# Residual block on one core: input transform for two channel blocks at a time, one more chunk by columns, single positions accumulated in the weight banks

## The chip, the core and the metric

The kernel runs on one core of one Trainium2 chip. A core has a matrix engine (TensorE, PE in the profile, with its weight loads as PEld), a vector engine (VectorE, DVE), an activation engine (ScalarE, ACT), a general engine (GpSimd, POOL) and a queue engine for transfers (SyncE, SP). They run side by side and wait for each other by semaphores. [...] The metric is the time of one execution on the device, in microseconds, as the median of several runs.

## What is computed

A residual block of a diffusion model, on two images of 512 channels and 64 x 64 points, in bf16:

```python
def conv3(z, w):
    zp = jnp.pad(z, ((0, 0), (0, 0), (1, 1), (1, 1)))
    taps = [jnp.einsum("bchw,oc->bohw", zp[:, :, i:i+H, j:j+W], w[:, :, i, j]) for i in range(3) for j in range(3)]
    return sum(taps)
h = conv3(silu(gn(x, g1, be1)), w1)          # gn: group norm, 4 groups of 128 channels
h = h + (silu(t_emb) @ w_emb).reshape(B, C, 1, 1)
h = conv3(silu(gn(h, g2, be2)), w2)
return x + h
```

Both convolutions have 512 input and 512 output channels: four blocks of 128 each way. "Layer one" and "layer two" below are the two convolutions.

## The kernel before

**Method.** Each convolution is done by a Winograd transform over rows: six rows of the input give six transformed rows (positions 0 to 5), and six products with transformed weights give four output rows. In the direction of columns there are two ways. By taps, a position is the sum of three matmuls per input block, one per column tap, each 512 columns wide (eight rows of 64). By columns, the row transform is followed by a second transform over pairs of columns: then a position is four products, each 256 wide, one matmul per input block. By taps a position takes 3 x 512 columns per input block, by columns 4 x 256.

**Tiling.** The 64 rows of an image make two chunks of 32 rows; with two images a layer has four chunks, numbered 1 to 4 here (idx 0 to 3 in the code). A *set* is one output block of one chunk: `one_set` (line 801), and `final_set` (line 747) for the very last. A set runs positions 1 and 3, then 0 and 5 (components 1 and 2), then 2 and 4, then the remaining components of 0 and 5; ACT evacuates each accumulator and DVE combines the results into the output rows `y`. Accumulators are three tiles `acc` of two banks each; two more banks, `xa` and `xb`, take the transposed weights. Positions 0 and 5 go by columns in all chunks but the first of layer one. Positions 1 and 3 go by columns in chunks 3 and 4 of layer two: `more_cols` (line 699) for chunk 3 and `more_pair` (line 734) for chunk 4.

**Input transform.** `v_block` (line 629) makes the transformed input V of one input block for one chunk. It loads the rows into one of two buffers `src`, ACT writes Silu of the normalised rows into one of two padded buffers `a_tmp` (rows of 66: a zero column on each side), and `make_v` (line 591) makes the positions: rows of 66 are read and written whole, so the sums have 1056 elements (2 x 8 x 66). For positions 0 and 5 by columns, one difference of 1024 and two sums of 512 that read every second element follow. `v_more_split` (line 557) and `v_more` (line 548) make the parts for positions 1 and 3 by columns. V has eight tiles, four per chunk in turn: the V of chunk n+2 is written when chunk n's sets are done.

**Weight transform.** `u_blocks` (line 493) loads weights, transposes them on PE into `xa` and `xb`, copies them out on ACT and makes the transformed weights U on DVE, in six sums per pair of blocks. `u_more` (line 475) turns the weights of positions 1 and 3 into those by columns, in place, after the last set that uses them by taps: now after chunk 2 of layer two.

**Order.** Nothing runs in program order. Every instruction is recorded with a cost and its dependencies, and a planner (class `_Plan`, line 25) makes one list per engine before the kernel is built, by forward and backward passes over the whole block with perturbed priorities; `STEPS` (line 31) lists the seeds of the perturbations that are kept. So the order of instructions on every engine can differ between two versions of the kernel even where the code is the same. Helper `tt` (line 316) records DVE's two-input operations and `act` (line 335) ACT's, which is why so many rows of the profile have lines L318 and L348; `groups` (line 659) records the matmuls (L667).

**Transfers.** SP issues loads, the store of layer one's output to memory (`h_scr`) and the stores of the result; POOL issues the transfers that add x to `y`.

Of the kernel before, what the change touches and what calls it, by code (L numbers as in the profile page):

```python
# [24 lines left out]
class _Plan:  # L25
# [5 lines left out]
    STEPS = ((0, 3), (500001, 2), (500002, 3), (500004, 3), (500005, 3), (500006, 3), (500007, 3), (500008, 2),  # L31
# [157 lines left out]
def kernel(  # L189
# [40 lines left out]
    COL0 = (1, 2, 3)  # L230
    SLOT = (1, 3, 2, 4, 0, 5)
# [30 lines left out]
    a_tmp = [sb([(CR + 2) * WP], f"a_tmp{i}") for i in range(2)]  # L262
    vt = sb([2, TR, 2, WP], "vt")
# [4 lines left out]
    Vbuf = [sb([VSZ], f"V{i}") for i in range(2 * CT)]  # L268
    src = [sb([(CR + 2) * W], f"src{i}") for i in range(2)]
    stage = [sb([CQ], f"stage{i}") for i in range(3)]  # L270
    stg = [sb([CR * W], f"y{i}") for i in range(3)]
    g1t = sb([TR * P], "g1t")
# [220 lines left out]
    def u_blocks(layer, ot, c0, loads, tmp=None, dve=False, act_scale=True):  # L493
# [4 lines left out]
        mid = slots(U, c0, n, S_MID, [[1, KP]])  # L498
        half = view(tmp, 0, [[KP, n], [1, KP]])
        up = lambda j: slots(U, c0, n, S_UP + NKX * j, [[1, KP]])  # L500
        for i, wn in enumerate(loads):
# [20 lines left out]
            copy(one(S_MID, 1), pb, "xb", KP, lambda t: t[:].rearrange("p k o -> p (k o)"))  # L522
        scaled(up(3), g(0), 0.25, act_scale and not dve)
        scaled(half, mid, 0.5, act_scale and not dve)
        tt(up(1), g(0), g(1), ALU.add)
        tt(up(0), up(1), mid, ALU.add)
        tt(up(1), up(1), mid, ALU.subtract)
        tt(up(3), up(3), g(1), ALU.add)
        tt(up(2), up(3), half, ALU.add)
        tt(up(3), up(3), half, ALU.subtract)  # L530
# [15 lines left out]
    more_buf = lambda ct: (a_tmp + src)[ct]  # L546

    def v_more(V, X):
        rows = lambda kx, st: view(V, kx, [[NI, 2], [WP, TR], [st, W // st]])
        dst = lambda o, n: view(X, o, [[n * TR, 2], [n, TR], [1, n]])  # L550
        tt(dst(0, W), rows(0, 1), rows(2, 1), ALU.subtract)
        tt(dst(4 * NC, W // 2), rows(1, 2), rows(2, 2), ALU.add)
        tt(dst(6 * NC, W // 2), rows(2, 2), rows(1, 2), ALU.subtract)

    spare = lambda ct: (stage + [g1t])[ct]

    def v_more_split(V, at, D):
        rows = lambda kx, st: view(at, kx, [[NI, 2], [WP, TR], [st, W // st]])
        tt(view(D, 0, [[W * TR, 2], [W, TR], [1, W]]), rows(0, 1), rows(2, 1), ALU.subtract)
        dst = lambda i: view(V, i * NI, [[NC, 2], [W // 2, TR], [1, W // 2]])  # L560
        tt(dst(0), rows(1, 2), rows(2, 2), ALU.add)
        tt(dst(1), rows(2, 2), rows(1, 2), ALU.subtract)

    def rhs_more_split(V, D, j, c):
        if c in (0, 3):
            return view(D, j * 2 * NC + (1 if c == 3 else 0), [[W, TR], [2, W // 2]])
        return view(V, (c - 1) * NI + j * NC, [[1, NC]])
# [4 lines left out]
    def rhs_row(V, pos, kx):  # L572
        return view(V, SLOT.index(pos) * NI + kx, [[WP, TR], [1, W]])

    def rhs_col(V, j, c, o=4 * NI):
        if c in (0, 3):
            return view(V, o + j * 2 * NC + (1 if c == 3 else 0), [[W, TR], [2, W // 2]])
        return view(V, o + (4 if c == 1 else 6) * NC + j * NC, [[1, NC]])

    def silu_rows(layer, b, ch, ct, res, at):  # L580
        rows = at[:].rearrange("p (r w) -> p r w", w=WP)
        r0 = ch * CR - 1
        lo, hi = max(r0, 0), min(r0 + CR + 2, H)
        for edge, r in ((ch == 0, 0), (ch == NCH - 1, CR + 1)):
            if edge:
                pool(lambda r=r: nc.gpsimd.memset(rows[:, r, 1:W + 1], 0.0), [], [rows[:, r, 1:W + 1]], cost=0.2)  # L586
        act(rows[:, lo - r0:hi - r0, 1:W + 1], res[:, lo * W:hi * W].rearrange("p (r w) -> p r w", w=W)
            if res.shape[1] == HW else res.rearrange("p (r w) -> p r w", w=W),
            func=ACT.Silu, bias=nb_all[layer, b][:, ct:ct + 1], scale=sc_all[layer, b][:, ct:ct + 1])

    def make_v(V, at, rs, col, on_act, split=False):
        n2 = 2 * NI
        q2 = view(vt, 0, [[2 * WP, TR], [1, 2 * WP]])
        s2 = view(vt, n2, [[2 * WP, TR], [1, 2 * WP]])
        s_, r_ = (view(vt, n2 + i * WP, [[2 * WP, TR], [1, WP]]) for i in range(2))
        qs, pr = (view(vt, i * WP, [[n2, 2], [2 * WP, TR], [1, WP]]) for i in range(2))
        rows2 = lambda j: view(at, j * WP, [[TH * WP, TR], [1, 2 * WP]])
        pair = lambda j, d: view(at, j * WP, [[d * WP, 2], [TH * WP, TR], [1, WP]])
        flat = lambda t, i: view(t, i * NI, [[WP, TR], [1, WP]])
        vv = lambda i: view(V, 2 * i * NI, [[NI, 2], [WP, TR], [1, WP]])  # L600
        scaled(q2, rows2(1), 4.0, on_act[0])
        tt(s2, rows2(3), rows2(1), ALU.subtract)
        tt(q2, q2, rows2(3), ALU.subtract)
        scaled(flat(rs, 0), r_, 0.25, on_act[1])
        scaled(flat(rs, 1), s_, -4.0, on_act[1])
        scaled(s_, s_, 2.0, on_act[2])
        if not split:
            tt(vv(0), pr, qs, ALU.add)
        tt(vv(1), pr, qs, ALU.subtract)
        if not col:  # L610
            w05 = view(V, 4 * NI, [[1, n2]])
            tt(view(V, 4 * NI, [[NI, 2], [WP, TR], [1, WP]]), pair(0, 5), pair(2, 1), ALU.subtract)
            tt(w05, w05, view(rs, 0, [[1, n2]]), ALU.add)
            return
        vt_, vo = (rs, n2) if split else (vt, 0)
        tt(view(vt_, vo, [[NI, 2], [WP, TR], [1, WP]]), pair(0, 5), pair(2, 1), ALU.subtract)
        if split:
            tt(view(at, 0, [[NI, 2], [WP, TR], [1, WP]]), pr, qs, ALU.add)
        w05f = view(vt_, vo, [[1, n2]])
        tt(w05f, w05f, view(rs, 0, [[1, n2]]), ALU.add)  # L620
        o = 4 * NI
        tt(view(V, o, [[W, 2 * TR], [1, W]]), view(vt_, vo, [[WP, 2 * TR], [1, W]]),
           view(vt_, vo + 2, [[WP, 2 * TR], [1, W]]), ALU.subtract)
        odd = view(vt_, vo + 1, [[WP, 2 * TR], [2, W // 2]])
        evn = view(vt_, vo + 2, [[WP, 2 * TR], [2, W // 2]])
        tt(view(V, o + 4 * NC, [[W // 2, 2 * TR], [1, W // 2]]), odd, evn, ALU.add)
        tt(view(V, o + 6 * NC, [[W // 2, 2 * TR], [1, W // 2]]), evn, odd, ALU.subtract)

    def v_block(layer, b, ch, ct, V, res=None, rs=None, on_act=(False, True, True)):
        at = a_tmp[count["v"] % 2]  # L630
        k = src[count["v"] % 2]
        count["v"] += 1
        r0 = ch * CR - 1
        lo, hi = max(r0, 0), min(r0 + CR + 2, H)
        if res is None:
            res = k[:, 0:(hi - lo) * W]
            from_h = layer == 1
            dma(res, (h_scr if from_h else x_v)[b, ct][:, lo * W:hi * W],
                reads=[f"h{b}{ct}{c}" for c in range(NCH)] if from_h else [], writes=[res])
        silu_rows(layer, b, ch, ct, res, at)  # L640
        split = layer == 1 and b * NCH + ch == len(chunks) - 2
        make_v(V, at, rs if rs is not None else k, is_col(layer, b, ch), (layer == 1,) + on_act[1:], split)
        if split:
            v_more_split(V, at, spare(ct))
# [33 lines left out]
    def row_pair(pair, U, V, gid):  # L678
        a = next_acc()
        todo = []  # L680
        for i, pos in enumerate(pair):
            for ct in range(CT):
                taps = [(u_tap(U[ct], pos, kx), rhs_row(V[ct], pos, kx)) for kx in range(NKX)]
                todo.append((i, a[:, i], [t[0] for t in taps], [t[1] for t in taps], 0.218 * NKX))
        groups(todo, a, (gid, pair))
        return a

    def col_pair(cc, U, V, gid, lead=0.0, js=(0, 1)):
# [3 lines left out]
        for j in js:  # L692
            for k, c in enumerate(cc):
                pairs = [(u_col(U[ct], j, c), rhs_col(V[ct], j, c)) for ct in range(CT)]
# [4 lines left out]
    def more_cols(U, V, gid):  # L699
        def cols(cc):  # L700
# [3 lines left out]
            for j in range(2):  # L704
                for k, c in enumerate(cc):
                    pairs = [(u_col_more(U[ct], j, c), rhs_more_split(V[ct], spare(ct), j, c)) for ct in range(CT)]
# [395 lines left out]
```

## Time and profile before

| | |
|---|---|
| median of 3 runs | 490.44 us (490.42 to 490.81) |
| profiled execution | 491.79 us |
| its span, first to last instruction | 489.7 us |
| mean granted clock of PE | 0.997 |
| busy: PE, weight loads, DVE, ACT, POOL | 481.4, 292.3, 459.6, 391.7, 46.7 us |
| chain of waits: PE, DVE, transfers | 91%, 5%, 2% |

How to read it: the busy time of an engine is the union of its instructions' records. Records of following instructions overlap, so that the time an instruction takes from its engine is read from start to start in the order of time, and not from its record. The slices show the busy share in forty equal parts of the span. The chain of waits is followed back from the last instruction to what released each step. In the groups, "x" is a count, and the numbers behind the bar are busy time, mean time of one in ns, and idle time of the engine just before them with what ended it.

### The profile page before, as it was taken

The page shows a single profiled execution, that of the slowest core. Times are in us where ns is not written, and L with a number is a line of the kernel's source. Part 1 is how long each engine was busy: PE and PEld are TensorE (multiplying, and loading weights), DVE is VectorE, ACT ScalarE, POOL GpSimd, SP SyncE. Part 2 cuts the span into 40 slices and gives each one's busy share as a digit, 9 for nine tenths or more (in the row PEclk, how much of TensorE's full clock was granted, in tenths as well). Part 3 has the DMA queues.
Part 4 walks back from the last instruction along what each step waited for, and adds up shares of the span by engine and source line. Part 5 has one row for each costly group of instructions (what it writes and reads, how often), then busy time and mean ns, then how long its engine had stood idle before and what let it go on. Part 6 is the DMA issues. An engine that isn't in the chain of part 4 may idle for free.

```text
span 489.7 us, 8717 instructions
## 1 busy us (share of the span) xinstructions
PE 481.4 (98%) x3273; PEld 292.3 (60%) x3273; DVE 459.6 (94%) x1000; ACT 391.7 (80%) x537; POOL 46.7 (10%) x102
## 2 busy tenths in 40 slices
PE   7999999999999999999999999999999999999996
PEld 7855544464655656566666555555555666767664
DVE  2799999999999999999999999999999999999576
ACT  1599999999978789999999899767769677627353
POOL 2210000011310004000000000410000000000000
PEclk9899999999999999999999999999999999999999
DMA  8534302851111243316433131354355536432544
GB/s 311 184 98 118 112 21 81 279 219 43 47 43 44 89 121 97 113 46 193 140 110 111 51 127 17 114 139 123 86 135 128 132 96 153 98 87 55 143 106 128
DMA packets 17316, 55.54 MB, mean 113 GB/s; under 512 B 1915, under 2 KB 3067, under 8 KB 16507
## 3 DMA queue, kind: packets, MB, share of 16 engines
q1 hardware_dynamic: 14912, 46.86, 28.3%
q0 software_dynamic: 2160, 7.87, 9.9%
q8 instruction: 25, 0.41, 0.3%
q10 hardware_dynamic: 203, 0.27, 0.2%
q14 instruction: 16, 0.13, 0.1%
HBM read 38.22 MB, written 16.78 MB: 112 GB/s over the span
## 4 chain that ended last, share of the span: by engine, by line
PE 91%; DVE 5%; DMA 2%; POOL 0%; ACT 0%; SPq 0%; issue 0%; DVEq 0%
PE acc L667 87%; PE xa L387 2%; DMA V<-in_x_dram 2%; DVE V L318 1%; DVE y L318 1%; PE xb L387 1%; PE acc L980 1%; DVE vt L318 1%; POOL arena L446 0%; SPq L366 0%; DVE stage L318 0%; DVE m L318 0%; DVE U L318 0%; PE acc L982 0%; ACT vt L348 0%
## 5 line engine op out<-in xcount | busy, mean ns | idle before, releaser
L667 PE MATMUL acc<-V,U 128*128 128x512 bf16 (+2 forms) x2416 | 434.5, 337 | 0.4 <-DVE V L318 0.3
L667 PEld LDWEIGHTS <-U 128*128 128x128 bf16 x2608 | 250.6, 98 | 176.6 <-issue 0.9
L318 DVE TENSOR_TENSOR V<-vt 128x1056 bf16<-128x1056 bf16 (+2 forms) x132 | 88.0, 690 | 0.4
L348 ACT ACTIVATE m<-w 128x512 bf16<-128x512 bf16 x62 | 37.5, 627 | 16.5 <-DVE w L318 16.4
L348 ACT ACTIVATE mb<-acc 128x1024 bf16<-128x1024 f32 x32 | 32.6, 1017 | 19.9 <-PE acc L667 13.7
L318 DVE TENSOR_TENSOR w<-m,w 128x1024 bf16<-128x1024 bf16 (+1 forms) x63 | 42.8, 680 | 2.3 <-ACT w L348 1.7
L318 DVE TENSOR_TENSOR U<-U 128x768 bf16<-128x768 bf16 (+2 forms) x96 | 44.2, 483 | 0.1
L348 ACT ACTIVATE w<-acc 128x1024 bf16<-128x1024 f32 (+1 forms) x32 | 32.3, 1008 | 14.1 <-PE acc L667 11.8
L348 ACT ACTIVATE a_tmp<-src,arena 128x2112 bf16<-128x2112 bf16 x20 | 42.9, 2145 | 0.0
L318 DVE TENSOR_TENSOR vt<-a_tmp 128x1056 bf16<-128x1056 bf16 x56 | 39.1, 699 | 0.7 <-ACT a_tmp L348 0.2
L348 ACT ACTIVATE src<-vt 128x528 bf16<-128x528 bf16 x54 | 34.1, 638 | 4.4 <-DVE vt L318 4.3
L518 ACT COPY U<-xa 128x768 bf16<-128x768 bf16 x31 | 24.9, 805 | 8.5 <-PE xa L387 8.4
L348 ACT ACTIVATE y<-y 128x2048 bf16<-128x2048 bf16 x16 | 30.6, 1918 | 1.0 <-DMA h_scr<-y 1.0
L387 PEld LDWEIGHTS <-stage 128*128 128x128 bf16 x288 | 25.9, 143 | 9.2
L348 ACT ACTIVATE a_tmp<-V,arena 128x2112 bf16<-128x2112 bf16 x12 | 25.9, 2158 | 3.5 <-DVE arena L331 3.5
L348 ACT ACTIVATE m<-acc 128x1024 bf16<-128x1024 f32 x24 | 24.4, 1018 | 5.2 <-DVE y L318 4.3
L318 DVE TENSOR_TENSOR sd<-mb 128x512 bf16<-128x512 bf16 x64 | 25.3, 415 | 3.3 <-ACT mb L348 3.3
L586 POOL MEMSET a_tmp<- 128x64 bf16 x32 | 5.8, 182 | 229.4 <-DVE vt L318 195.0
L366 POOL DMA_DIRECT2D y<-in_x_dram x15 | 13.2, 880 | 132.9 <-DVE y L318 119.6
L318 DVE TENSOR_TENSOR y<-m,w 128x1024 bf16<-128x1024 bf16 x31 | 21.2, 684 | 3.1 <-ACT m L348 2.7
L318 DVE TENSOR_TENSOR y<-sd,acc 128x512 bf16<-128x512 bf16 (+1 forms) x34 | 21.9, 686 | 1.2 <-PE acc L667 0.8
L348 ACT ACTIVATE src<-V 128x2048 bf16<-128x2048 bf16 x12 | 22.9, 1907 | 0.0
(125 smaller groups left out, 509.8 us busy)
## 6 DMA issues: line engine op xcount, KB each, us to landing
stage<-in_w_dram SPq DMA_DIRECT2D x32, 288.0 KB, 2.9
src<-h_scr SPq DMA_DIRECT2D x16, 528.0 KB, 3.8
h_scr<-y SPq DMA_DIRECT2D x16, 512.0 KB, 2.9
y<-in_x_dram POOLq DMA_DIRECT2D x15, 512.0 KB, 5.5
out_dram<-y SPq DMA_DIRECT2D x15, 512.0 KB, 2.6
V<-in_x_dram SPq DMA_DIRECT2D x6, 1024.0 KB, 7.0
src<-in_x_dram SPq DMA_DIRECT2D x4, 528.0 KB, 4.0
V<-in_x_dram SPq DMA_DIRECT2D x4, 512.0 KB, 6.4
```

Of the source, the lines that this page charges most:

```text
L318: lambda: nc.vector.tensor_tensor(out=out, in0=in0, in1=in1, op=op), [in0, in1], [out], **kw)
L348: nc.scalar.activation(out=out, in_=in_, func=fn, scale=scale, **extra)
L366: q.dma_start(out=out, in_=in_, **extra)
L387: nc.tensor.transpose(sel(t), in_, ident[:in_.shape[0], :in_.shape[0]])
L518: lambda: nc.scalar.copy(out=out, in_=sel(bank.get())), [tok], [out])
L586: pool(lambda r=r: nc.gpsimd.memset(rows[:, r, 1:W + 1], 0.0), [], [rows[:, r, 1:W + 1]], cost=0.2)
L667: nc.tensor.matmul(ap, lhsT=l, rhs=r, start=k == 0, stop=k == total[key] - 1)
L980: nc.tensor.matmul(gr, lhsT=blk, rhs=blk, start=(k == 0 and j == 0), stop=(k == 1 and j == 15))
```

## The change

1. Chunk 2 of layer two also does positions 1 and 3 by columns (`MORE = 1`, an index from 0), with `more_cols`; `u_more` follows chunk 1 instead of chunk 2. The column parts of chunks 2 and 3 lie in two places in turn (`d_part`), and for that the y buffers are three in number with other places, two in chunk 2.
2. The input transform handles two input blocks in one instruction (`v_block` with n = 2); only chunk 1 of layer one still goes block by block. There is one padded buffer `at` and one `src2` for the pair. V has four tiles of a pair each. Borders are left out of the sums (rows of 64 instead of 66, from the second element on), and POOL zeroes V's border columns (`pads`). The odd and even columns are separated first (`sp`), by ACT in chunks 2 to 4 of layer two and by DVE elsewhere, so that the sums over columns read neighbouring elements.
3. In chunks 2 to 4 of layer two positions 2 and 4 accumulate one by one in the weight banks `xa` and `xb` (`row_lone`) instead of together in an `acc` tile, and are evacuated one by one.
4. Layer two's weight transform makes its sums two slots at a time (`wide`): three sums of 1536 for six of 768.
5. The planner's seeds are others (73 steps for 44).

```diff
+    LONE = 1
+    ACT_SPLIT = (1, 2, 3)
+    MORE = 1
-    a_tmp = [sb([(CR + 2) * WP], f"a_tmp{i}") for i in range(2)]
-    vt = sb([2, TR, 2, WP], "vt")
+    at = sb([2 * (CR + 2) * WP], "at")
-    Vbuf = [sb([VSZ], f"V{i}") for i in range(2 * CT)]
+    Vbuf = [sb([2 * VSZ], f"V{i}") for i in range(CT)]
+    src2 = sb([2 * (CR + 2) * W], "src")
...
+        if wide:
+            scaled(up(2), g(0), 0.25, act_scale)
+            scaled(half, mid, 0.5, act_scale)
...
+            tt(a, d4(U, base(0), (S_UP + 2 * NKX) * P, NSL * P), d4(U, base(S_G2), 0, NSL * P), ALU.add)
+            mh = d4(tmp, n * KP, -n * KP, KP)
+            tt(d4(U, base(S_UP + NKX), 2 * KP, NSL * P), a, mh, ALU.subtract)
+            tt(a, a, mh, ALU.add)
...
+    def v_more_split(V, R, idx, c0):
+        D, o, step = d_part(idx, c0)
+        rows = lambda kx, st: view(R, kx, [[2 * NI, 2], [WP, 2 * TR], [st, W // st]])
+        tt(view(D, o, [[step, 2], [W, 2 * TR], [1, W]]), rows(0, 1), rows(2, 1), ALU.subtract)
+        dst = lambda i: view(V, i * 2 * NC, [[2 * NI, 2], [W // 2, 2 * TR], [1, W // 2]])
         tt(dst(0), rows(1, 2), rows(2, 2), ALU.add)
         tt(dst(1), rows(2, 2), rows(1, 2), ALU.subtract)
...
+    def pads(V, n):
+        o = view(V, 0, [[WP, n], [WP - 1, 2]])
+        pool(lambda: nc.gpsimd.memset(o, 0.0), [], [o], cost=0.3)
+
+    def v_block(layer, b, ch, c0, n, Vs, res=None, on_act=(False, True, True), clean=False):
...
+        for c in range(n):
+            ct = c0 + c
+            act(view(at, A + (lo - r0) * row + c * WP + 1, [[row, hi - lo], [1, W]]),
+                got[c].rearrange("p (r w) -> p r w", w=W), func=ACT.Silu, bias=nb_all[layer, b][:, ct:ct + 1],
+                scale=sc_all[layer, b][:, ct:ct + 1])
+        if clean:
+            pads(V, 8 * TR)
+        split = layer == 1 and MORE <= idx < len(chunks) - 1
...
+        rows2 = lambda j: view(at, A + j * row + 1, [[TH * row, TR], [WP, 2 * n], [1, W]])
...
+        vv = lambda i: view(V, i * IN + (c0 % 2) * 2 * NI + 1, [[WP, 2 * TR], [2 * NI, n], [1, W]])
+        scaled(q2, rows2(1), 4.0, layer == 1)
         tt(s2, rows2(3), rows2(1), ALU.subtract)
         tt(q2, q2, rows2(3), ALU.subtract)
...
+        if layer == 1 and idx in ACT_SPLIT:
+            w = view(R, w05 + 1, [[WP, rows], [1, W]])
+            tt(w, w, view(R, 0, [[W, rows], [1, W]]), ALU.add)
+            act(sp, apart(w05 + 1, WP))
+        else:
+            tt(sp, apart(w05 + 1, WP), apart(0, W), ALU.add)
+        each = lambda i: view(at, so + i, [[WP, rows], [HP, 2], [1, W // 2]])
+        one = lambda i: view(at, so + i, [[WP, rows], [1, W // 2]])
+        dst = lambda k: view(V, OUT + k * 4 * NC, [[W // 2, rows], [1, W // 2]])
+        tt(view(V, OUT, [[W // 2, rows], [4 * NC, 2], [1, W // 2]]), each(0), each(1), ALU.subtract)
+        tt(dst(2), one(HP), one(1), ALU.add)
+        tt(dst(3), one(1), one(HP), ALU.subtract)
         if split:
-            v_more_split(V, at, spare(ct))
+            v_more_split(V, at, idx, c0)
...
+    def row_lone(pos, U, V, gid, out, scales=(KAPPA,)):
+        tag = ("xa", "xb")[pos // 4]
+        bank, done = XBank(tag, [NFREE], F32), [0]
+        taps = [(u_tap(U[ct], pos, kx), rhs_row(V, ct, pos, kx)) for ct in range(CT) for kx in range(NKX)]
...
+        for o, f in zip(out, scales):
+            plan.add("ACT", 0.09 + NFREE * 0.00081, lambda o=o, f=f: nc.scalar.activation(
+                out=o, in_=bank.get()[:], func=ACT.Copy, scale=f), [tag], [o])
...
-        more = layer == 1 and idx >= len(chunks) - 2
+        more = layer == 1 and idx >= MORE
+        few = layer == 1 and MORE < len(chunks) - 2 and idx <= MORE
+        yst = next_y(2 if few and idx == MORE else 3, few)
...
-                if layer == 1 and idx == len(chunks) - 3:
+                if layer == 1 and idx == MORE - 1:
                     for c0 in range(0, CT, 2):
                         u_more(1, ot, c0, 2)
...
-                    for ct in range(CT):
-                        v_block(*tgt, ct, Vs[ct])
+                    for c0 in range(0, CT, 2):
+                        v_block(*tgt, c0, 2, Vs, clean=layer == 1 and idx == len(chunks) - 3 and MORE < len(chunks) - 2)
```

More of the change, by code (lines that the diff above doesn't have):

```diff
@@ L555, with rhs_more @@
[L555 to L560, printed above, removed]
+        tt(dst(8 * NC, W // 2), rows(1, 2), rows(2, 2), ALU.add)
+        tt(dst(12 * NC, W // 2), rows(2, 2), rows(1, 2), ALU.subtract)
+    def rhs_more(ct, j, c):
+        X, row = ((at, src2)[ct // 2], (ct % 2) * 2 + j)
+        if c in (0, 3):
+            return view(X, row * 2 * NC + (1 if c == 3 else 0), [[W, TR], [2, W // 2]])
+        return view(X, ((8 if c == 1 else 12) + row) * NC, [[1, NC]])
@@ L582, in silu_rows @@
         r0 = ch * CR - 1
         lo, hi = max(r0, 0), min(r0 + CR + 2, H)
+        got = []
+        for c in range(n):
+            ct = c0 + c
+            if res is None:
+                got.append(src[ct % 2][:, 0:(hi - lo) * W])
+                from_h = layer == 1
+                dma(got[c], (h_scr if from_h else x_v)[b, ct][:, lo * W:hi * W],
+                    reads=[f"h{b}{ct}{k}" for k in range(NCH)] if from_h else [], writes=[got[c]])
+            else:
+                got.append(res[ct][:, lo * W:hi * W])
@@ L584, in silu_rows @@
         for edge, r in ((ch == 0, 0), (ch == NCH - 1, CR + 1)):
             if edge:
[L586 to L601, printed above, removed]
+                o = view(at, A + r * row + 1, [[WP, n], [1, W]])
@@ L616, in make_v @@
-        tt(view(vt_, vo, [[NI, 2], [WP, TR], [1, WP]]), pair(0, 5), pair(2, 1), ALU.subtract)
+        w05 = 4 * TR * W
+        rows = 4 * TR
+        tt(view(R, w05, [[WP, 2 * TR], [2 * NI, 2], [1, WP]]), pair(0, 5), pair(2, 1), ALU.subtract)
+        so = 0
         if split:
[L618 to L642, printed above, removed]
+            so = 4 * NI
```

196 lines of the change are left out of this document (117 added, 79 removed), and 14 rows, old and new, of the table STEPS.

## The prediction

> **What bounds the kernel now.** I read the page's busy shares and slices first, then the chain of waits, then the engines' queues in order of time, and last the waits just before the end.
>
> ```profile
> span 489.7 us, 8717 instructions
> PE 481.4 (98%) x3273; PEld 292.3 (60%) x3273; DVE 459.6 (94%) x1000; ACT 391.7 (80%) x537; POOL 46.7 (10%) x102
> ...
> DVE  2799999999999999999999999999999999999576
> ACT  1599999999978789999999899767769677627353
> ...
> PE 91%; DVE 5%; DMA 2%; POOL 0%; ACT 0%; SPq 0%; issue 0%; DVEq 0%
> ...
> L667 PE MATMUL acc<-V,U 128*128 128x512 bf16 (+2 forms) x2416 | 434.5, 337 | 0.4 <-DVE V L318 0.3
> ```
>
> PE carries 91% of the chain, and its convolution group sat idle for 0.4 us in all. DVE is at nine tenths or more from slice 3 to slice 37, so it is nearly a second bound. ACT is full only in the first third and around slices 20 to 25. A busy PE need not be a PE at its peak, so its pace is checked in stretches of the chain in order of time:
>
> ```profile
> 60.08 23.55 PE acc L667 x108
> ...
> 302.91 170.55 PE acc L667 x1109
> ```
>
> The first stretch lies in layer one's first chunk, where every matmul is 512 wide: 23.55 / 108 = 0.218 us each. The second, by the order of the kernel's matmuls, holds 441 of 512 and 668 of 256 columns: (170.55 - 441 x 0.218) / 668 = 0.111 us for one of 256. Width sets the time, and nothing stands between the matmuls: PE is the bound from about 34 us to the tail.
>
> How close is DVE? Two views, DVE's and PE's queue near the place where the last chunk's products by columns are made:
>
> ```profile
> 441.75 0.68 DVE L318 TENSOR_TENSOR a_tmp<-V 128x512 bf16<-128x512 bf16 x1
> ```
>
> ```profile
> 442.76 0.38 PE L667 MATMUL acc<-a_tmp,U 128*128 128x256 bf16 x2
> ```
>
> The last such part is written at 442.43, and PE's next pair that reads this tile starts at 442.76. DVE delivers with a few tenths to spare, so a change that only took PE work away would be given back at once. What DVE pays decides.
>
> **The change part by part.** Durations of DVE are taken from start to start in its queue, since the records overlap:
>
> ```profile
> 344.73 0.42 DVE L318 TENSOR_TENSOR sd<-mb 128x512 bf16<-128x512 bf16 x1
> 345.06 0.70 DVE L318 TENSOR_TENSOR a_tmp<-vt 128x1056 bf16<-128x1056 bf16 x1
> 345.68 0.70 DVE L318 TENSOR_TENSOR V<-vt 128x1056 bf16<-128x1056 bf16 x1
> 346.30 0.68 DVE L318 TENSOR_TENSOR V<-a_tmp 128x512 bf16<-128x512 bf16 x1
> 346.90 0.68 DVE L318 TENSOR_TENSOR stage<-a_tmp 128x1024 bf16<-128x1024 bf16 x1
> 347.51 0.68 DVE L318 TENSOR_TENSOR V<-a_tmp 128x512 bf16<-128x512 bf16 x1
> ```
>
> 1056 contiguous elements take 0.62, 1024 take 0.61, 512 take 0.33; 512 read with a stride of two take 0.60. So an instruction costs some 0.07 us and 0.52 ns an element, and 1.04 ns where it strides. Larger sizes are estimated along these lines: 2048 cost 1.14, 2112 cost 1.17, 1024 strided 1.14, 2048 strided 2.20, 1536 cost 0.87.
>
> 1. *Chunk 2 of layer two by columns (MORE = 1).* In each of its four sets, positions 1 and 3 are 24 matmuls of 512 now and become 32 of 256: 24 x 0.218 - 32 x 0.111 = 1.68 us, times four 6.7 us off PE. The upper bound of the 256-wide price is that of sets that already go this way:
>
> ```profile
> 404.78 0.50 PE L667 MATMUL acc<-stage,U 128*128 128x256 bf16 x3
> ...
> 406.60 4.58 PE L667 MATMUL acc<-V,U 128*128 128x512 bf16 x34
> ```
>
> The 16 matmuls from 404.78 to 406.60 take 0.114 each, which gives 6.3 us. I take 6.5. On DVE the same edit adds, for two channel pairs, one difference of 2048 and two strided of 1024 (2 x 3.4 us), and in each set two sums of 512 and two evacuations from PSUM:
>
> ```profile
> L331 DVE SCALAR_TENSOR_TENSOR m<-acc,sd 128x512 bf16<-128x512 f32 x8 | 5.3, 721 | 0.0
> ```
>
> at most 0.72 each, so 4 x (2 x 0.33 + 2 x 0.72) = 8.4 us; in all some 15 us of new DVE work. The weights for it (three sums of 512 and one scaling per pair, some 1.2 us, eight pairs) move from chunk 2 into chunk 1; the count of DVE's lead below has them in their new place.
>
> 2. *Input transform for two blocks at a time.* In layer two a pair costs now twice (six of 1056, one of 1024, two strided of 512): 2 x (3.72 + 0.61 + 1.20) = 11.1 us. After, it is five of 2048, one of 2112, another of 2048 and two of 1024: 5.7 + 1.2 + 1.1 + 1.2 = 9.2 us, as the de-interleaving copy goes to ACT in three of the four chunks (where it stays on DVE, 2.20 takes the place of 1.14). Counted over the whole order of both kernels with the prices above, all DVE forms together: 188 fewer of 1056 (-116), 48 fewer of 768 against 24 of 1536 (-2), 72 fewer strided of 512 (-43), 82 of 2048 (+93), 14 of 2112 (+16), 20 larger strided (+31), the rest +14: about 7 us less in spite of the 15 added.
>
> 3. *The de-interleaving on ACT* adds six copies of 2048, and the lone rows split eleven evacuations of 1024 into 22 of 512:
>
> ```profile
> L348 ACT ACTIVATE w<-acc 128x1024 bf16<-128x1024 f32 x31 | 31.7, 1021 | 13.1 <-PE acc L667 10.8 <-DVE y L318 1.8 <-ACT y L348 0.3
> L348 ACT ACTIVATE y<-y 128x2048 bf16<-128x2048 bf16 x16 | 30.6, 1918 | 1.0 <-DMA h_scr<-y 1.0
> ...
> L348 ACT ACTIVATE vt<-acc 128x512 bf16<-128x512 f32 x18 | 9.7, 595 | 6.0 <-PE acc L667 5.2 <-DVE m L318 0.6
> ```
>
> That is 6 x 1.92 = 11.5 and 22 x 0.60 - 11 x 1.02 = 2 us, in chunks where ACT has room:
>
> ```profile
> 90.00:120.00 30.00, 30.00 (x176) 16.28 (x175) 29.79 (x65) 29.89 (x40) 4.26 (x9) 1.00 0.45 164
> ...
> 420.00:450.00 30.00, 30.00 (x223) 21.45 (x222) 29.69 (x54) 16.50 (x25) 1.72 (x2) 1.00 0.36 79
> 450.00:480.00 30.00, 30.00 (x204) 19.63 (x203) 20.81 (x38) 15.10 (x25) 2.59 (x3) 1.00 0.47 116
> ```
>
> (busy time of PE, weight loads, DVE, ACT, POOL). At 420 ACT works 16.5 of 30 us, so both count nothing; from 90 to 120, where it is full, nothing is added. If the cover were gone they would cost those 13 us.
>
> 4. *Lone rows in the weight banks.* The same matmuls write another bank; no column is added. Worth nothing on a PE that waits 0.4 us; what it frees are accumulators.
>
> 5. *Wide weights, fewer y buffers, zeroed borders.* The weights' temporary now belongs to a pair until its column sums are done; the saved 2 us are in the count above. In chunk 2 two y buffers turn instead of three: a set's y is busy for its add and its store, 5.5 and 2.6 us after issue, against two sets of over 11 us. Border memsets move to V and are of the kind at 0.2 us on an engine that is 10% busy.
>
> ```profile
> src<-h_scr SPq DMA_DIRECT2D x16, 528.0 KB, 3.8
> ...
> y<-in_x_dram POOLq DMA_DIRECT2D x15, 512.0 KB, 5.5
> out_dram<-y SPq DMA_DIRECT2D x15, 512.0 KB, 2.6
> ```
>
> 6. *Start.* Until 34 us DVE's transforms for the first chunk stand in the chain (the wait at 33.97 is for V). Their rows lose two border columns, 1056 to 1024, 0.01 to 0.02 us each in some 24 instructions; I take 0.2 us, with bounds of -0.5 and +0.5 because the interleaving with the norms is new.
>
> ```profile
> 33.97 0.81 PE L667 MATMUL acc<-V,U 128*128 128x512 bf16 x3 [0.34 <-DVE V L318]
> ```
>
> *Does DVE still deliver?* Adding up each queue in the two orders: DVE's work up to its last product for the last chunk falls from 417.6 to 413.9 us, and PE's work ahead of the first matmul that reads it goes from 422.9 to 423.6. The lead grows by 4.4 us; if DVE idles as it does now, the few tenths above become some 4 to 5 us. So PE keeps the saving.
>
> One cost has no row. The new views start at odd elements (the border column is left out; the halves of a split row are 33 apart): in the new order 124 two-input instructions of DVE, over 204,800 elements, read or write at an odd element, and in the present order none. They price at 0.52 ns an element if the start does not matter, 1.04 if it halves the rate. I take the first, since rows of 64 at a stride of 256 (the y writes of 1024) already cost as much as contiguous ones. [...]
>
> The sum, against the profiled execution's own time of 491.79 (span 489.7 and 2.1 around it): 491.8 - 6.5 - 0.2 = 485.1. The runs' median, 490.44, lies 1.35 below that execution, so the forecast is 490.44 - 6.7 = 483.8.
>
> **The rivals.**
>
> *DVE gives part of it back* (0.09). The pair has one input buffer, where two took turns. From its release a load (3.8) and two Silu instructions must pass before DVE can begin the pair:
>
> ```profile
> L348 ACT ACTIVATE a_tmp<-src,arena 128x2112 bf16<-128x2112 bf16 x20 | 42.9, 2145 | 0.0
> ```
>
> 3.8 + 2 x 2.1 = 8 us, in which DVE needs other work. The new order puts 10 to 20 us of DVE work between load and first use in layer two, which speaks against it; that the loads queue on SP behind stores speaks for it. With 1 us lost per pair over the eight pairs of layer two, DVE is 8 us late, 4 more than its lead: 487.8; range 485.5 to 489.4.
>
> *Slower, by the odd starts* (0.08). DVE has 4 to 5 us of lead and PE 6.7 us of saving. From 11.5 / 204,800 = 0.056 ns an element on (11% of 0.52) the kernel is slower than now; at a quarter more, 0.13 ns, by 27 - 11.5: 506; at half rate 107 us more, 586. For it: no row shows such a start. Against it: the price per element has been the same for every even view here, with rows or without.
>
> *The change does nothing* (0.03): DVE, not PE, would pace layer two in both kernels. Then DVE's 4.4 us of new lead is all there is and is spent on waits for ACT's copies: 490. Against it stands PE's pace of 0.218 and 0.111 through 170 us without a gap.
>
> **How the numbers follow.** Forecast 0.80 at 483.8, own range 482.3 to 485.3 (6.3 or 6.7 for PE, half a microsecond of start either way, another half for records). The rivals take 0.09, 0.08 and 0.03. A change of 0.2% (1 us) is about what a measurement of this kernel can tell. Faster 0.80 + 0.08 of the first rival = 0.88; same 0.03; slower 0.09. The range goes from 482.0 to 487.8: it leaves out the far half of the first rival and the others, about 0.16.
>
> **What would show it.** PE's convolution group has 96 fewer of 512 and 128 more of 256 and still idles under 1 us; DVE's rows of 2048 last about 1.2 us by their records, whether they start odd or even; the last products for chunk 4 come some microseconds ahead of PE. Rows of 2048 above 1.4 us, or PE waiting for DVE V in layer two, make it wrong.

## The result, and the profile after

The changed kernel runs in 487.94 us (median of 5 runs, 486.92 to 489.28). The ratio to the kernel before is 0.9945, with a 95% interval of 0.9927 to 0.9964: 2.7 us less (1.8 to 3.6), where 6.7 were forecast and where the range ended at 487.8. Differences below are worked out in the same way, as ratio times 490.44 us, because the kernel before itself was timed again beside each group of runs (490.4 to 491.7); nearly all have an interval of about 1 us to either side.

The page of the changed kernel:

```profile
span 486.6 us, 8586 instructions
...
PE 474.2 (97%) x3305; PEld 294.3 (60%) x3305; DVE 456.1 (94%) x848; ACT 398.0 (82%) x510; POOL 44.4 (9%) x95
...
DVE  2899899999999989799999999999999999999976
ACT  1799999999987869799999999958759397973653
...
L719 PE MATMUL acc<-V,U 128*128 128x512 bf16 (+2 forms) x2096 | 363.3, 326 | 2.9 <-DVE V L330 1.0
```

PE's busy time fell by 7.2 us, from 481.4 to 474.2: the columns did go away. But the span less PE's busy time rose from 489.7 - 481.4 = 8.3 to 486.6 - 474.2 = 12.4 us, so 4.1 us came back as idle time of PE: 3.1 of them between 40 and 480 us, 0.9 ahead of 40. DVE's busy time is 3.5 us less than before, and DVE is at nine tenths or more in every slice from the eighteenth to the thirty-eighth. The chain of waits of this execution breaks off after 8% of the span and says nothing. What PE waits for is read from its waits between 40 and 480 us (total, times, longest); the kernel before has none there:

```profile
PE acc L719 <- ACT m L360: 0.8, 2, 0.5
PE acc L719 <- ACT mb L360: 0.6, 2, 0.5
PE acc L719 <- DVE V L330: 0.5, 1, 0.5
PE acc L719 <- DVE y L330: 0.4, 2, 0.2
PE xa L750 <- ACT w L755: 0.3, 1, 0.3
PE acc L719 <- DVE arena L330: 0.2, 1, 0.2
PE acc L719 <- DVE spare L330: 0.2, 1, 0.2
```

Only one of the ten waits is put down to an operand (V). Eight others end with an instruction of ACT or DVE that empties an accumulator (m, mb and w of ACT; y and spare of DVE), and the one put down to arena comes right behind four DVE instructions that read acc. PE is seldom short of input; it wants to write where the last product has not been fetched yet.

The lead of the operands has not grown either. The last product by columns for the last chunk is written at 447.05, and the next pair on PE that reads this tile starts at 447.15; the prediction had it some microseconds ahead.

```profile
445.83 1.22 DVE L330 TENSOR_TENSOR at<-V 128x1024 bf16<-128x1024 bf16 x1
```

```profile
447.15 0.38 PE L719 MATMUL acc<-at,U 128*128 128x256 bf16 x2
```

### The profile page after: what moved, and what is told of

Read it like the earlier page. It is cut to its first block, busy times and chain, and to the rows that moved or that the text cites. A ratio compares the mean times of both kernels' runs of the same rounds, so it can differ in the third digit from the quotient of the medians.

```text
span 486.6 us, 8586 instructions
## 1 busy us (share of the span) xinstructions
PE 474.2 (97%) x3305; PEld 294.3 (60%) x3305; DVE 456.1 (94%) x848; ACT 398.0 (82%) x510; POOL 44.4 (9%) x95
## 5 line engine op out<-in xcount | busy, mean ns | idle before, releaser
L719 PE MATMUL acc<-V,U 128*128 128x512 bf16 (+2 forms) x2096 | 363.3, 326 | 2.9 <-DVE V L330 1.0
L330 DVE TENSOR_TENSOR V<-at 128x2048 bf16<-128x2048 bf16 (+2 forms) x68 | 67.1, 1003 | 2.3 <-ACT at L360 2.1
L360 ACT ACTIVATE at<-src,arena 128x2112 bf16<-128x2112 bf16 x20 | 43.6, 2207 | 7.8 <-DVE V L330 6.0
L750 PE MATMUL xa<-V,U 128*128 128x512 bf16 x144 | 37.1, 381 | 0.3 <-ACT w L755 0.3
L750 PE MATMUL xb<-V,U 128*128 128x512 bf16 x144 | 37.3, 381 | 0.0
L330 DVE TENSOR_TENSOR U<-U 128x768 bf16<-128x768 bf16 (+3 forms) x72 | 35.1, 507 | 0.3
L399 PEld LDWEIGHTS <-spare 128*128 128x128 bf16 x288 | 25.4, 143 | 9.0
L360 ACT ACTIVATE at<-V,arena 128x2112 bf16<-128x2112 bf16 x12 | 26.1, 2191 | 5.1 <-DVE arena L343 4.6
L330 DVE TENSOR_TENSOR V<-V 128x2048 bf16<-128x2048 bf16 x24 | 28.9, 1222 | 0.0
L360 ACT ACTIVATE src<-V 128x1024 bf16<-128x1024 bf16 x24 | 24.9, 1052 | 0.7 <-DVE V L330 0.6
```

The lines of the kernel that those rows point to most:

```text
L330: lambda: nc.vector.tensor_tensor(out=out, in0=in0, in1=in1, op=op), [in0, in1], [out], **kw)
L360: nc.scalar.activation(out=out, in_=in_, func=fn, scale=scale, **extra)
L399: nc.tensor.transpose(sel(t), in_, ident[:in_.shape[0], :in_.shape[0]])
L719: nc.tensor.matmul(ap, lhsT=l, rhs=r, start=k == 0, stop=k == total[key] - 1)
L750: nc.tensor.matmul(bank.get()[:], lhsT=taps[i][0], rhs=taps[i][1], start=done[0] == 1, stop=done[0] == len(taps))
```

## The experiments

**The theories.** A: rows that DVE reads from an odd element cost more than the planner and the forecast counted, DVE comes late by some 3.5 us, and PE waits. B: DVE loses its lead between 160 and 215 us, where the pair has one buffer and DVE idles 6 us, and layer two lacks that time. C: PE's waits have nothing to do with DVE. D, formed on the waits above: what counts is not how far operands are ahead but how early accumulators are emptied, and there neither kernel has room.

### Even sources

```diff
...
-lambda: nc.vector.tensor_tensor(out=out, in0=in0, in1=in1, op=op)
+lambda: nc.vector.tensor_tensor(out=even(out) if same(out, in0) else out, in0=even(in0), in1=even(in1), op=op)
```

> The changed kernel with every source of DVE that starts at an odd element read one element earlier, from an even one; the order on all engines is the same. What is computed is not the block any more: the sums take neighbouring elements. In the trace of the changed kernel a source of 2048 in rows of 64 that starts odd takes 1.169 us from start to start, where one that starts even takes 1.136; that is 1 ns a row, 3.5 us in all, 1.7 of it after 220 us. Theory A (the odd rows make DVE late and PE wait for it): the rows come down to 1.136, and the median falls from 487.9 by 3 to 3.5, to 484.7. Theory B (DVE loses its lead in the second half of layer one, where one pair buffer lets no load run ahead, and has to catch up): only the odd rows behind that place count, 487.9 - 1.7 = 486.2, and DVE still waits at 201 us. Theory C (PE's 5.9 us of waits after 40 us do not come from DVE): 487.9.

Measured: 486.29 us, ratio 0.9887 (0.9870 to 0.9903), 5.5 us under the kernel before and 2.8 under the changed one. DVE's instructions by form, mean of one in ns behind the comma; the changed kernel:

```profile
L330 DVE TENSOR_TENSOR V<-at 128x2048 bf16<-128x2048 bf16 x28 | 35.5, 1269 | 2.2 <-ACT at L360 2.1
L330 DVE TENSOR_TENSOR V<-at 128x1024 bf16<-128x1024 bf16 x36 | 29.3, 829 | 0.1
L330 DVE TENSOR_TENSOR V<-V 128x2048 bf16<-128x2048 bf16 x24 | 28.9, 1222 | 0.0
...
L330 DVE TENSOR_TENSOR V<-V,at 128x2048 bf16<-128x2048 bf16 x14 | 17.5, 1252 | 0.1
L330 DVE TENSOR_TENSOR src<-src 128x2048 bf16<-128x2048 bf16 x6 | 7.5, 1251 | 0.0
```

and with even sources:

```profile
L339 DVE TENSOR_TENSOR V<-at 128x2048 bf16<-128x2048 bf16 x28 | 34.1, 1218 | 1.9 <-ACT at L369 1.8
L339 DVE TENSOR_TENSOR V<-V 128x2048 bf16<-128x2048 bf16 x24 | 28.8, 1218 | 0.0
L339 DVE TENSOR_TENSOR V<-at 128x1024 bf16<-128x1024 bf16 x36 | 28.3, 800 | 0.1
...
L339 DVE TENSOR_TENSOR V<-V,at 128x2048 bf16<-128x2048 bf16 x14 | 17.0, 1215 | 0.1
L339 DVE TENSOR_TENSOR src<-src 128x2048 bf16<-128x2048 bf16 x6 | 7.3, 1212 | 0.0
```

Those that read odd rows get shorter by 29 to 51 ns (28 x 51 + 36 x 29 + 14 x 37 + 6 x 39 ns = 3.2 us); V<-V, whose sources start even in both kernels and whose destination starts odd in both, stays. PE's waits between 40 and 480 us fall from 3.0 to 0.8 us:

```profile
PE acc L728 <- DVE V L339: 0.5, 1, 0.5
PE acc L728 <- ACT m L369: 0.3, 1, 0.3
```

What follows: C falls, and A is borne out. The gain of 2.8 us, with about 1.2 to either side, is nearer to A's 3 to 3.5 than to B's 1.7 but does not exclude the latter, so B is tried by itself.

### Six loads left out, alone and with even sources

```diff
...
+            if skip:
+                return
...
+                    skip=(layer, idx, c0) in ((0, 3, 2), (1, 0, 0), (1, 0, 2)))
```

> The changed kernel without six loads of the input rows: those of the second channel pair of layer one's chunk 4 and of both pairs of layer two's chunk 1, issued between 160 and 215 us. Those pairs are computed from what lies in the buffer. The order on all engines is the same. Theory A (odd rows): no load matters, 487.9. Theory B (late pairs): the load of 4 to 5 us that stands between the last read of the buffer and the next Silu is gone; ACT's waits of 3.2 us at 179 and 1.7 us at 197 and DVE's of 1.6 us at 201 shrink to nothing, and some 3 us of lead reach layer two: 485, with fewer waits of PE after 240. Theory C (PE's waits do not come from DVE): 487.9.

> Both edits together, even sources and six loads left out. A and B both: DVE is no longer late, PE's waits after 40 us, 5.9 us in the changed kernel, go below 1.5, and the median comes to 483 to 484, which is the time forecast. A alone: as the run with even sources. B alone: as the run without the loads. C: 487.9.

Measured: 488.22 us, ratio 0.9946 (0.9927 to 0.9966), 2.6 under the kernel before: nothing gained over the changed kernel. With even sources 486.14 us, 0.9893 (0.9876 to 0.9910), 5.2 under: nothing gained over even sources alone. In its first form B falls: the wait of 1.6 us at 201 stays. What ACT's Silu waits for between 160 and 215 us without the loads is still DVE, which must be done with the padded buffer:

```profile
ACT at L360 <- DVE V L330: 4.9, 2, 3.2
```

### Nothing between two pairs

```diff
...
+            o, i = (out[:, 0:2], in_[:, 0:2]) if short else (out, in_)
...
+            short = (layer, idx, c0) in ((0, 3, 2), (1, 0, 0), (1, 0, 2))
...
```

> The changed kernel without the six loads and with the six Silu instructions behind them cut to 2 rows of 33, so that next to nothing stands between DVE's last read of the pair's padded buffer and its work on the next pair, in layer one's last and layer two's first chunk. The order on all engines is the same; those pairs are computed from old data. The changed kernel ran 2.7 us under the kernel before. Theory B in its second form (it is the one padded buffer, not the load, that makes DVE idle there, and the idle time is what layer two lacks): the waits of DVE between 160 and 215 us, 6 us in five places, go below 2, the lead is there in layer two, and the time comes to 5 to 6 us under the kernel before, as with even sources. Theory A alone (the odd rows decide, and DVE's idle time in layer one is time it could not use): within 0.7 us of the changed kernel, though the waits are gone.

Measured: 487.56 us, ratio 0.9919 (0.9896 to 0.9943), 4.0 under the kernel before, between the two expectations: 1.3 less than the changed kernel, with intervals that overlap. DVE's waits from 160 to 215 us, in the changed kernel:

```profile
DVE src L330 <- issue: 1.6, 1, 1.6
DVE y L330 <- ACT m L360: 1.5, 1, 1.5
DVE y L343 <- PE acc L719: 1.2, 1, 1.2
DVE aux L330 <- ACT m L360: 0.8, 1, 0.8
DVE V L330 <- ACT at L360: 0.8, 1, 0.8
```

and in this run:

```profile
DVE y L330 <- ACT m L361: 1.5, 1, 1.5
DVE y L343 <- PE acc L724: 1.2, 1, 1.2
DVE w L330 <- ACT w L361: 1.0, 1, 1.0
DVE V L330 <- ACT at L361: 0.8, 1, 0.8
DVE aux L343 <- PE acc L724: 0.5, 1, 0.5
```

They fall from 5.9 to 5.0 us only. The wait of 1.6 us for the pair is gone, and DVE waits longer for ACT's and PE's results instead, which are what the other waits end with too. So the one buffer is a small part of this idle time. Whether the 1.3 us are real stays open.

### More work for DVE, in the changed kernel and in the kernel before

```diff
...
-        tt(sd[:, 0], mb[:, 0], mb[:, 1], ALU.add)
+        tt(sd[:, 0], mb[:, 0], mb[:, 1], ALU.add, times=3 if idx == 1 else 1)
```

In the kernel before it is `times=3`, since there only chunk 3 runs this line.

> The changed kernel with 2.65 us of DVE work added: in each set of layer two's chunk 2 the sum of 512 in the step by columns is done three times, 8 x 0.33 us, between 330 and 370 us. Same result, same order. If DVE paces the kernel from 240 to 440 us (theories A and B): 487.9 + 2.65 = 490.5, the whole of the gain over the kernel before. If PE does and DVE is on time (theory C): 487.9 to 488.3.

> The kernel before with the same 2.65 us of DVE work added as in the changed kernel: in each set of the chunk that does positions 1 and 3 with the step by columns (chunk 3, between 370 and 420 us) the sum of 512 is done three times. Same result, same order. In the changed kernel this work cost 4 us and more. As the forecast read the lead (operands written 1.9 to 2.5 us ahead of PE until 420 us, 0.4 at 442.8): 2.65 - 0.4, so 2.2 us slower. Theory D (PE waits for accumulators that DVE or ACT must empty, so the lead on operands says little): either clearly less than 2 us, if the accumulators have room here, or more than 2.65, if they have none.

Measured: 492.86 us, ratio 1.0034 (1.0011 to 1.0058), 1.7 us over the kernel before and so 4.4 over the changed one (about 1.5 to either side); and 494.11 us, ratio 1.0078 (1.0058 to 1.0098), 3.8 over the kernel before (2.8 to 4.8).

The work added was more than the 2.65 us expected. At the same place the changed kernel has two sums sd, and this run four:

```profile
380.72 0.76 DVE L330 TENSOR_TENSOR sd<-mb 128x512 bf16<-128x512 bf16 x2
381.39 0.68 DVE L330 TENSOR_TENSOR y<-y,w 128x1024 bf16<-128x1024 bf16 x1
```

From start to start the two take 0.67 us; the four, shown below, take 1.59. An add that is followed by the same add takes 0.43 to 0.48 us, where a single one takes 0.335, so that 3.7 us were added over the four sets, in both kernels. What slows them the traces do not show. So the work was paid in full both times, to within the intervals: no room for it shows in either kernel. How PE comes to wait is seen in the first of the two, in order of time:

```profile
383.35 1.67 DVE L330 TENSOR_TENSOR sd<-mb 128x512 bf16<-128x512 bf16 x4
384.94 0.68 DVE L330 TENSOR_TENSOR y<-y,w 128x1024 bf16<-128x1024 bf16 x1
...
385.72 0.60 ACT L756 ACTIVATE w<-xa 128x512 bf16<-128x512 f32 x1 [3.60 <-DVE y L330]
...
386.37 1.01 PE L751 MATMUL xa<-V,U 128*128 128x512 bf16 x3 [2.09 <-ACT w L756]
```

ACT may not empty bank xa into w until DVE has added the old w to y; until then PE may not write xa. In the changed kernel the same wait of PE is the 0.3 us in the list above. The kernel before, with the extra work, shows waits of the same kind where it had none:

```profile
PE acc L668 <- DVE m L332: 1.2, 2, 0.9
PE acc L668 <- ACT mb L349: 1.0, 2, 0.7
```

The 4.4 us of the changed kernel hold something else as well. Right behind PE's wait of 2.09 us, from 386.9 to 390.3, PE was granted half its clock: 13 matmuls take 3.38 us there, and by an estimate half of the 3.40 us, 1.7 us, is what the clock costs (the view gives busy time of PE, weight loads, DVE, ACT and POOL, then the granted clock):

```profile
386.90:390.30 3.40, 3.38 (x13) 1.59 (x12) 3.40 (x5) 0.33 (x1) 0.00 (x0) 0.50 0.83 133
```

The changed kernel's clock stays at 1.00 until 480 us. The twelve executions with the extra work had a mean granted clock of 0.995 (0.999 in the five of the changed kernel): the four with 0.998 or more took 491.1 to 492.2 us, the others 492.4 to 498.2. That the wait brought the lower clock on is not shown.

What follows: D, as far as it says where PE waits. Between 40 and 480 us none of PE's waits in these two runs is put down to an operand; all end as accumulators are emptied. For the kernel before, the cost alone does not decide: the 0.4 us of lead that the prediction read there would have left 3.3 of the 3.7, which is within the interval.

### The buffer moved by one element

```diff
-    at = sb([2 * (CR + 2) * WP], "at")
+    at = sb([2 * (CR + 2) * WP + 2], "at")[:, 1:2 * (CR + 2) * WP + 1]
...
-        w05 = 4 * TR * W
+        w05 = 4 * TR * W + 1
```

> The changed kernel with its padded buffer moved by one element, so that the 64 points of a row start at an even address, and the place of the scratch for positions 0 and 5 moved by one as well. The result is the block, the order is the same. Odd rows that DVE reads go from 3.46 us to 1.43 us, at 1.04 ns each. With even sources everywhere 3.46 us less of DVE work made the time 2.4 us shorter than that of the changed kernel; theory A expects the same share here, 1.4 us: 4.1 us under the kernel before. If the gain of even sources came from anything else that the shifted reads changed: 2.7 under it, as the changed kernel.

Measured: 487.44 us, ratio 0.9902 (0.9881 to 0.9923), 4.8 under the kernel before: 2.1 less than the changed kernel for 2.0 us of odd rows, a little more than expected. The same forms again:

```profile
L330 DVE TENSOR_TENSOR V<-at 128x1024 bf16<-128x1024 bf16 x36 | 28.3, 799 | 0.1
...
L330 DVE TENSOR_TENSOR src<-at 128x2112 bf16<-128x2112 bf16 x14 | 17.8, 1272 | 1.3 <-issue 1.3
```

The sums of 1024 are as short as with even sources, while forms that now start odd get longer: src<-at, of 16 rows, goes from 1252 to 1272 ns.

### New lists, with and without the measured prices

```diff
...
+        odd = max(odd_rows(a) for a in aps[1:]) * 0.00104
...
-            return 0.08 + n * (0.00051 if fast else 0.00102)
+            return 0.07 + odd + n * (0.00052 if fast else 0.00104)
```

The lists of all engines are made anew with other seeds. The control has the new seeds only.

> The changed kernel, its computation untouched, with the list of each engine made anew from prices that hold the odd rows (1.04 ns each) and the measured strided instructions, 3.9 us more of DVE work than the planner counted. Theory A in its wider form (DVE's work in layer two fits, but the lists were made for a DVE that is 3.9 us faster, and accumulators are emptied late because of it): PE's waits of 5.9 us after 40 us shrink to under 2.5 and the time comes to 5.5 to 6 us under the kernel before, though DVE does as much work as now. If DVE has no room left at all: 2.7 under it, as the changed kernel.

> The control for the run with new lists: the changed kernel, its computation untouched, with lists made anew by the same search, but from the planner's old prices, which hold no odd rows. If the measured prices are what the run with new lists gained by (theory A in its wider form): as the changed kernel, 2 to 3.5 us under the kernel before, against 5.1 for that run. If any new search finds better lists: 5 us under, the same within half a microsecond.

Measured: with the measured prices 486.83 us, ratio 0.9896 (0.9877 to 0.9914), 5.1 under the kernel before; with the old prices 488.31 us, 0.9953 (0.9938 to 0.9969), 2.3 under, as the changed kernel. The computation is the same in all three, and DVE is busy for 455.8, 456.3 and 456.1 us. So DVE's work fits beside PE's, odd rows and all. What cost the time is that the order was written out for a DVE that is 3.9 us faster than the real one: 3.5 us of odd rows, the rest other prices. The control's search kept fewer seeds (475 for 993), but that is not the reason: by the planner's own reckoning, each with its own prices, both lists end at 479.0 us. It is still one list of each kind. With the measured prices 1.6 of the 1.8 us that PE still waits between 40 and 480 us are put down to V: once accumulators are emptied in time, operands come next.

### Both: moved buffer and new lists

> The shifted buffer and the new lists together: 2 us less of DVE work, and lists that know what is left. Theory A: PE's waits after 40 us below 2 us, the time 6 to 6.7 us under the kernel before, which is the gain that was forecast. If the new lists alone already leave PE no wait: the same as those within 0.5 us.

> The shifted buffer with other new lists, made for DVE instructions that take 1% more than measured, so that there is room for waits that no price holds. If what was left of PE's waits in the run with shifted buffer and new lists (2 us after 40) is due to lists without room: those waits go below 1 us and the time is 7 us under the kernel before. If they are of another kind: the same within 0.7 us of that run, 6.5 under.

Measured: 484.55 us, ratio 0.9868 (0.9845 to 0.9891), 6.5 us under the kernel before, the fastest of all and close to the gain that was forecast; with prices 1% above the measured ones 485.20 us, 0.9873 (0.9845 to 0.9900), the same, with no fewer waits: its traced execution, the longest of the six at 486.94 us, has 3.6 us of them. The page of the first:

```profile
span 482.8 us, 8594 instructions
...
PE 473.3 (98%) x3305; PEld 294.9 (61%) x3305; DVE 454.1 (94%) x848; ACT 397.4 (82%) x510; POOL 41.7 (9%) x95
```

and its waits of PE between 40 and 480 us:

```profile
PE xb L851 <- DVE V L431: 0.5, 1, 0.5
PE xb L1067 <- DMA spare<-in_w_emb_dram: 0.2, 1, 0.2
PE acc L820 <- DVE m L444: 0.2, 1, 0.2
```

The span less PE's busy time is 9.5 us (12.4 in the changed kernel), and 0.9 us of waits are left of 3.0.

### Parts of the change taken back

Each has lists made anew from the measured prices, so they are compared with the run of that kind, 5.1 us under the kernel before.

```diff
-    MORE = 1
+    MORE = 2
```

> The changed kernel with chunk 2 of layer two back by taps (MORE = 2), all else as changed, with lists made anew from the measured prices as in the run with new lists. PE has 6.7 us more, DVE 14 us less. If PE's columns are what the change is worth and the other parts nothing (as forecast): 6.7 us over the run with new lists, which ran 5.1 under the kernel before, so 1.6 us over the kernel before, or the same within a microsecond. If the other parts gain by themselves on DVE's side: 1 to 3 us under the kernel before.

```diff
-    LONE = 1
+    LONE = 4
```

> The changed kernel with positions 2 and 4 back in one accumulator tile in all chunks (LONE = 4, the last set excepted), lists made anew from the measured prices. PE and DVE have the same work. By the forecast's step on lone rows (worth nothing): as the run with new lists, 5.1 us under the kernel before. Theory D (what PE waits for is an accumulator that ACT or DVE has not emptied yet, and three tiles must then serve four pairs of positions instead of three in each set): 1 to 3 us under the kernel before, with PE's waits in layer two ended by evacuations.

```diff
-    ACT_SPLIT = (1, 2, 3)
+    ACT_SPLIT = ()
```

> The changed kernel with the de-interleaving back on DVE in all of layer two (ACT_SPLIT empty): six strided sums of 2.20 us in place of six even ones of 1.14 and of six ACT copies of 1.9; lists made anew from the measured prices. DVE has 6.4 us more, ACT 11 less. If DVE paces layer two: 4 to 6 us slower than the run with new lists, between 1 under and 1 over the kernel before. If DVE has the lead of 4 to 5 us that was forecast: at most 2 us slower, 3 to 5 under.

Measured: without the additional chunk by columns 491.83 us, ratio 1.0010 (0.9993 to 1.0027), 0.5 over the kernel before and 5.6 over the run compared with. Without lone rows 490.98 us, 1.0000 (0.9982 to 1.0018), 5.1 over it. With the de-interleaving on DVE 488.76 us, 0.9954 (0.9934 to 0.9973), 2.8 over it. So the columns are the gain, and the other parts together are worth nothing without them; but without lone rows none of it arrives. PE's waits without them, 40 to 480 us:

```profile
PE acc L852 <- DVE y L476: 2.1, 3, 0.9
PE acc L852 <- ACT mb L493: 1.5, 2, 1.0
PE acc L852 <- DVE y L463: 0.7, 1, 0.7
PE acc L852 <- DVE m L476: 0.3, 1, 0.3
PE acc L852 <- ACT w L493: 0.3, 1, 0.3
```

All 4.9 us end with an accumulator being emptied; the span less PE's busy time is 489.7 - 474.2 = 15.5 us. So two more banks in the rotation are worth 5 us here. The planner reckons with 3.4 of them: by it the lists end at 482.4 us without lone rows and 479.0 with them. One reservation: each of these three has lists of its own, and how good a list is may differ. Two pairs of runs in which little but the list differs lie 0.4 us apart (the changed kernel and the control) and 0.3 (the two with moved buffer), so that an effect of 1 us or less would not be told from it.

## Why the prediction was wrong

- **What bounds the kernel.** PE was read rightly as the bound, and DVE as close behind. How close was not: the few tenths at 442 us were only the lead of an operand, and PE waits for accumulators too.
- **Step 1, the columns: right.** PE's busy time fell by 7.2 us for 6.5 forecast; with new lists it is 6.3 less than without the columns in chunk 2, and taking them back costs 5.6 us. DVE's new work is as tallied too: from start to start the 22 instructions added take 8 x 0.62 + 8 x 0.335 + 6 x 1.135 = 14.5 us, for some 15. The net, 7 us less forecast and 3.5 measured, is off by the odd rows: with even sources DVE's busy time is 6.8 less than before.
- **The odd starts: the step that failed.** "I take the first" put them at the even price, 0.52 ns an element, as if the start did not matter. They cost about 1 ns for each row read (from start to start 1.169 against 1.136 us for 32 rows of 64 in the changed kernel): 3.2 us by the records, 3.46 as counted at 1.04 ns a row, which is 3.46 / 204,800 = 0.017 ns an element. Neither of the two ends given for the price was met, the truth lay close to the lower one, and the sum had no term for it. Even sources give back 2.8 of the 4.0 us that are missing.
- **The lead of 4 to 5 us: the second failed step, without which the first would have done no harm.** "The lead grows by 4.4 us" was counted from DVE's products to the matmuls that read them. By that count the odd rows would have left 0.9 us of lead and no wait; the trace has 3.0 us of waits, all but 0.5 at accumulators, which are emptied by DVE, or by ACT after DVE. No lead of that kind was found in either kernel: 3.7 us more of DVE work cost 3.8 us before, and 4.4 after with a lower clock. The list written out by the planner left none, and work that it did not price was paid in full.
- **Step 4, lone rows: wrong.** "Worth nothing on a PE that waits 0.4 us" judged them by the kernel before. In the new one, with four sets more that need four products by columns, they are worth 5 us.
- **Step 3, ACT:** that the copies cost nothing on ACT was not tried by itself. Back on DVE the same work, some 6 us of it, costs 2.8.
- **Steps 5 and 6** (wide weights, y buffers, start) were not tried alone. The 0.2 us at the start did not come: ahead of 40 us PE stands idle for 3.7 us before, 4.5 in the changed kernel and 3.3 with even sources, in one execution of each, so the odd rows cost time there too.
- **The signs named at the end.** Two came up: PE's convolution group stands idle for 2.9 us, not under 1, and PE waits for V in layer two (0.5 us). The third, rows of 2048 above 1.4 us, did not (1.25 to 1.27 in the groups shown); that mark was too high to show what went wrong.
- **The rivals.** The time came out at the first one's, 487.8, by chance and not by its way: six loads taken out changed nothing, and with the Silu behind them cut short as well 1.3 us were gained, which may be nothing. The second, slower by odd starts, had the right cause at the wrong size; its point of 0.056 ns an element rested on the lead that was not there. The third, in which DVE paces layer two in both kernels, was nearer to the truth than its 0.03: DVE work added in layer two was paid in full in both kernels, though its 490 was not reached. In the changed kernel it held for the order that was written, not for the work, as the new lists show.

## What to carry to other kernels

Where two engines are within a few per cent of each other, count the lead at every place where one can hold up the other: at the operands, and at the accumulators and buffers that must be emptied before they are written again. An order written out from prices is only as good as the prices: measure every new form of instruction after a change, put it into the prices, and make the order anew before the change is judged. Here that step alone, with no change to the computation, took the gain from 2.7 to 5.1 us, and one element of padding with it to 6.5.

## What the runs showed of the hardware

The DVE sums on bf16 in these kernels keep their rate when their sources start at an odd element, but take about 1 ns more for each row that starts so: in the changed kernel and with even sources 1251 against 1212 ns for 32 rows of 64 (src<-src), 829 against 800 for 32 rows of 32 (V<-at of 1024). A destination that starts odd costs nothing to speak of: V<-V, from even sources, takes 1.13 us from start to start in the changed kernel, as spare<-at does, which starts even on all sides. Of the two prices weighed in the prediction the even one, 0.52 ns an element, holds for the rate and for the destination, but not for the start of each row of a source; the rate is not halved.

The second thing not expected is that equal DVE sums of 512 elements in a row, each writing over the result of the last, take 0.43 to 0.48 us from start to start, where a single one takes 0.335. The cause stays open. The third is that a wait of PE stood right ahead of a lower clock: 2.09 us of waiting, then 3.4 us at a granted clock of 0.50, in one execution. That the one led to the other is not shown.
